# Two transformer layers on one core: key and value loads reordered, phi on GpSimd, and instruction order from a searched list

## The chip, the cores and the metric

The kernel runs on one core of a Trainium2 chip. The metric is device microseconds of one execution. Most executions of one kernel agree within about 0.3%. A profile is one execution, and its "span" is about 1.7 us shorter than the time reported for it.

## The reference

Two layers of a linear-attention block and a gated MLP, on x of 2048 x 512 in bf16:

```python
x = A_x
x = x + _A_ref(_layernorm(x), A_wqkv, A_w_phi, A_wo)      # layer 0
x = x + _B_ref(_layernorm(x), B_W_gate, B_W_up, B_W_down)
x = x + _A_ref(...)                                       # layer 1, same weights
x = x + _B_ref(...)
# _A_ref, 32 heads of 16: q, k, v; phi(k) = [softmax(k w), softmax(-k w)], the same for q;
#   o = phi(q) (phi(k)^T v) / (phi(q) sum(phi(k)));  o @ wo
# _B_ref: (relu(x Wg) * (x Wu)) Wd, with F = 1376
```

## The kernel before

The program is a list of about 2100 operations (`Op`), each with an engine, a cost, a "due" time and its dependences. At build time `plan` simulates the five engines with these costs and emits the operations in the order of the simulated start. Where several operations of an engine could start at the same moment, the one with the smallest due time goes first. `refine` makes the due times: it plans forward, then plans backward from the end, and takes how far before the end each operation must be done as its new due time, ten times over. So its due times are distances to the end along the critical path.

```python
XPOSE = (1200, 2430)       # a DMA transpose: issue, and ns until it has landed
def refine(ops, rounds):
    ...
    for k in range(rounds):
        dues = [o.due for o in ops]
        span = max(o.end for o in plan(ops))
        if best is None or span < best[0]:
            best = span, dues
        back(ops)          # due = -(time left to the end), planned backward
    ...
    return plan(ops)
```

A tile of 128 tokens goes through these steps in a layer (cut):

```python
# normalize (VectorE), then transpose by DMA (or by TensorE for a few early tiles)
xn = (x - mean) * rstd
nc.sync.dma_start_transpose(out=dst(), in_=src.t[:])          # XPOSE
# keys: K = xn^T Wk (4 matmuls of 512 columns), two exps (ScalarE), row sums (VectorE)
# phi = exp * 1/sum, on VectorE, GpSimd, or half each:
if phi_eng == "POOL":  phi(nc.gpsimd, 0, 2)
elif phi_eng == "DVE": phi(nc.vector, 0, 2)
else: phi(nc.vector, 0, 1); phi(nc.gpsimd, 1, 1)              # "BOTH"
# kvz: phi^T [V, 1] summed over all 16 tiles in PSUM
# attend: Eq R (erq), divide (VectorE), transpose o by DMA, output projection (proj), X += ...
# mlp: transpose by DMA, gate and up (G, Up), relu and copy (ScalarE), product (VectorE), down, X += ...
```

Before, phi of layer 0 is "BOTH" for every tile. The transposed tile is needed by TensorE for K, V, proj, G and Up, so a late transpose can stop TensorE.

The softmax here doesn't subtract the row's maximum and nothing guards it: scores larger than these inputs give would overflow.

Of the kernel before, what the change touches and what calls it, by code (L numbers as in the profile page):

```python
# [8 lines left out]
P = 128  # L9
D = 512  # L10
# [138 lines left out]
def back(ops):  # L149


    left = {o: len(o.then) + len(o.behind) for o in ops}
    ready = dict.fromkeys(ops, 0.0)
    clock = dict.fromkeys(HOP, 0.0)
    open_ = {e: [o for o in ops if o.eng == e and not left[o]] for e in HOP}
    for _ in ops:
        best = None
        for e, cand in open_.items():
            if cand:
                at = [(max(clock[e], ready[o] + o.end - o.start - o.spent), o) for o in cand]  # L160
                first = min(t for t, o in at)
                if best is None or first < best[0]:
                    best = first, max((o for t, o in at if t <= first + 1), key=lambda o: (o.start, o.n))
        t, o = best
        clock[o.eng] = t + o.spent
        o.due = -clock[o.eng]
        open_[o.eng].remove(o)
        for d in o.deps:
            left[d] -= 1
            ready[d] = max(ready[d], HOP[o.eng] - o.due)  # L170
            if not left[d]:
                open_[d.eng].append(d)
        for d in o.follow:
            left[d] -= 1
            ready[d] = max(ready[d], d.start + d.spent - d.end - o.due)
            if not left[d]:
                open_[d.eng].append(d)


def refine(ops, rounds):  # L180
    taker = {b: o for o in ops for b in o.takes}
    last = {}
    for o in ops:
        for b in o.takes:
            if b.pool.fifo:
                if b.pool in last:
                    o.follow.append(last[b.pool])
                last[b.pool] = o
    for n, o in enumerate(ops):
        o.n = n  # L190
        o.follow += {taker[b] for b in o.uses} - set(o.deps) - set(o.follow)
        for d in o.deps:
            d.then.append(o)
        for d in o.follow:
            d.behind.append(o)
    best = None
    for k in range(rounds):
        dues = [o.due for o in ops]
        span = max(o.end for o in plan(ops))
        if best is None or span < best[0]:  # L200
            best = span, dues
        back(ops)
    for o, due in zip(ops, best[1]):
        o.due = due
    return plan(ops)
# [4 lines left out]
def mm(n, cols):  # L210
    t = n * (cols / 2.4 + 2.5)
    return t, t + 170
# [24 lines left out]
XPOSE = (1200, 2430)  # L237
RATE = 265.0
# [15 lines left out]
ROUNDS = 10  # L254
BLOCKS = ((1, 1, 2, 2, 2, 2, 2, 2, 2), (1, 1, 2, 2, 2, 2, 2, 2, 1, 1))


@with_exitstack
def kernel(
# [22 lines left out]
    def x_of(t):  # L282
        return X[t // C][:, t % C, :]
# [42 lines left out]
    wqkv = A_wqkv.rearrange("(b p) f -> p b f", p=P)  # L326
    x_in = [None] * T
    x_in[0] = load(0, X[0][:, 0, :], xv[:, 0, :], 131072)
    l_wk = [load(0, wk[:, b:b + 2, :], wqkv[:, b:b + 2, D:2 * D], 262144, "ACT") for b in (0, 2)]
    l_wf = load(1, wf[:], A_w_phi.rearrange("(b j) d f -> (j d) b f", b=NB, j=8), 65536)  # L330
    x_in[1] = load(2, X[0][:, 1, :], xv[:, 1, :], 131072)
    l_wv = load(3, wv[:], wqkv[:, :, 2 * D:3 * D], 524288, "ACT")
    op("ACT", (1300, 1300), 5, lambda: nc.scalar.preload_act_table_set("natural_log_exp_and_others"), name="tbl")
    wov = A_wo.rearrange("(h bb c) f -> c h bb f", bb=NB, c=C)
    gv, uv = (w.rearrange("(b p) f -> p b f", p=P) for w in (B_W_gate, B_W_up))
    dv = B_W_down[0:10 * P, :].rearrange("(f p) d -> p f d", p=P)
    l_wq, l_wo, l_wg, l_wu, l_wd = [], [], [], [], []
    late = [("q", wq[:, b, :], wqkv[:, b, 0:D], 131072) for b in range(NB)]
    late += [("g", wg[:, b, :], gv[:, b, :], 352256) for b in range(NB)]
    late += [("o", wo[i * H:(i + 1) * H, :, :], wov[i], 131072) for i in range(C)]  # L340
    late += [("u", wu[:, b, :], uv[:, b, :], 352256) for b in range(NB)]
    late += [("d", wd[:, f:f + 2, :], dv[:, f:f + 2, :], 262144) for f in range(0, 10, 2)]
    late += [("d", wd[:96, 10, :], B_W_down[10 * P:F, :], 98304)]
    homes = dict(q=l_wq, g=l_wg, o=l_wo, u=l_wu, d=l_wd)

    def load_next(after, due):
        if late:
            kind, dst, src, nbytes = late.pop(0)
            homes[kind].append(load(due, dst, src, nbytes, follow=[after]))
# [29 lines left out]
    def fold(w, dst, loaded, due, step, engs):  # L379
# [10 lines left out]
        for m in range(NB):  # L390
            ps = Buf(p_b)
            f = op("PE", mm(4, 128), due + step + m, lambda m=m, ps=ps: [nc.tensor.matmul(
                ps.t[:, b * P:(b + 1) * P], lhsT=wT.t[:, b, m * P:(m + 1) * P], rhs=Wblk[:, b, :],
                start=True, stop=True) for b in range(NB)], [turned[m], c_blk] + turned[:m], [ps], [wT], name="fold")
            done.append(evac(engs[m % 2], due + step + m, lambda m=m: dst[:, m, :], lambda ps=ps: ps.t[:], [f], (),
                             [ps], "W2"))
# [5 lines left out]
    def turn(src, dst, how, due, after, takes, uses, name):  # L402
        if how == "SP":
            return op("SP", XPOSE, due, lambda: nc.sync.dma_start_transpose(out=dst(), in_=src.t[:]), [after],
                      takes, [src] + uses, name=name, move=500)
        ps = Buf(p_b)
        a = op("PE", mm(4, 128), due, lambda: [nc.tensor.matmul(
            ps.t[:, b * P:(b + 1) * P], lhsT=src.t[:, b * P:(b + 1) * P], rhs=ident[:], start=True, stop=True)
            for b in range(NB)], [after, c_id], [ps], [src], name=name)
        return evac(how, due, dst, lambda: ps.t[:].rearrange("p (b t) -> p b t", b=NB), [a], takes, [ps] + uses,  # L410
                    name)
# [7 lines left out]
    def norm_A(l, t, due, after, how):  # L419
# [11 lines left out]
        return turn(xn, lambda: xnTA[c][:, :, i * P:(i + 1) * P], how, due, n, [], [], "xnTA")  # L431


    class Keys:
# [6 lines left out]
        def tile(self, t, due, due_v, due_z, xT, phi_eng, v_eng="ACT"):  # L441
# [12 lines left out]
                for b in range(NB)], [xT, l_wv], [vp], name="V")  # L454
# [119 lines left out]
    def mlp(l, t0, n, due_x, due_g, due_d, after, how):  # L574
# [3 lines left out]
        turned = []  # L578
        for i in range(n):
            t = t0 + i  # L580
            a = stats(l, "B", t, due_x(i), [after[t]])
            xc = Buf(p_xn)
# [6 lines left out]
            out=tmp[:, t0:t0 + n], in0=mv[:, t0:t0 + n, 1], scalar1=EPS, scalar2=None, op0=Alu.add), [a], name="ve")  # L589
# [44 lines left out]
        for i in range(n):  # L634
            t = t0 + i
            yp = Buf(p_b)
            last = None
            for lo, hi in ((0, 4), (4, 8), (8, NF)):
                def down(yp=yp, i=i, lo=lo, hi=hi):
                    for f in range(lo, hi):  # L640
                        m = min(P, F - f * P)
                        nc.tensor.matmul(yp.t[:], lhsT=h.t[:m, f * W + i * P:f * W + (i + 1) * P],  # L642
                                         rhs=wd[:m, f, :], start=(f == 0), stop=(f == NF - 1))
                last = op("PE", mm(hi - lo, 512), due_d(i) + lo, down,
                          [made[f] for f in range(lo, hi)] + l_wd + ([last] if lo else []),
                          [] if lo else [yp], [yp, h] if lo else [h], name="down")
            x = x_of(t)
            done.append(op("DVE", dve(512, 1, 130), due_d(i), lambda x=x, yp=yp, t=t: nc.vector.scalar_tensor_tensor(  # L648
                out=x, in0=yp.t[:], scalar=rs[:, t:t + 1], in1=x, op0=Alu.mult, op1=Alu.add), [last, r], (), [yp],
                name="resB"))  # L650
# [6 lines left out]
    for t in range(T):  # L657
        if t == 2:
            x_in[2] = load(4, X[0][:, 2, :], xv[:, 2, :], 131072)
            x_in[3] = load(5, X[0][:, 3, :], xv[:, 3, :], 131072)  # L660
        if t >= 4 and t % 2 == 0:
            x_in[t] = x_in[t + 1] = load(
                p["K0"] + p["KS"] * (t - 5), X[t // C][:, t % C:t % C + 2, :], xv[:, t:t + 2, :], 262144,
                follow=[xT[t - 4]] if t > 6 else [])
        xT.append(norm_A(0, t, p["K0"] - 4000 + p["KS"] * t, [x_in[t]], ("ACT", "DVE")[t % 2] if t < 4 else "SP"))
        if t >= 3:
            load_next(xT[t], p["K0"] + p["KS"] * t)
            load_next(xT[t], p["K0"] + p["KS"] * t)
        k0 = p["K0"] + p["KS"] * t
        keys.tile(t, k0, k0 + p["V0"], k0 + p["Z0"], xT[t], "BOTH")  # L670
# [5 lines left out]
    for l in range(2):  # L676
# [18 lines left out]
        for t0, n, s0 in begin:  # L695
# [4 lines left out]
            for i, a in enumerate(done):  # L700
                t = t0 + i
# [5 lines left out]
                else:  # L707
                    op("SP", (460, 1700), e0, lambda t=t: nc.sync.dma_start(
                        out=ov[:, t, :], in_=x_of(t)), [a], name="store",
                       move=131072 / RATE)  # L710
        xT = nxt

    order = refine(ops, ROUNDS)
# [33 lines left out]
```

## Time and profile before

| | before |
|---|---|
| time | 402.70 us, median of 3 runs (402.51 to 403.94) |
| span of the profiled run | 401.2 us |
| TensorE at the measured matmul rates | 380 us of it |

The first lines of the page of the kernel before:

```profile
span 401.2 us, 8365 instructions
PE 387.8 (97%) x3176; PEld 265.9 (66%) x3176; DVE 275.5 (69%) x685; ACT 259.5 (65%) x704; POOL 22.1 (6%) x24
```

A busy TensorE is not yet a full one, since the records of pipelined matmuls overlap (one of 512 columns is recorded as 379 ns). So I use a second measure. In the chain of waits, matmuls in an unbroken row take 216 ns for 512 columns, 109 for 256, and 56 for 128. The sum of all matmuls at these rates, up to a moment, is subtracted from the time up to that moment; this difference is called **shortfall** below. Before, it is 17.8 us by 385 us, and it grows in the first 30 us (10.6), in 60 to 80 (2.7) and in 250 to 300 (2.4).

The busy time by stages, before (columns: window, then busy us and instruction count of TensorE, weight loads, VectorE, ScalarE and GpSimd, then granted clock, share of the DMA engines, GB/s):

```profile
10.00:20.00 10.00, 8.38 (x52) 4.16 (x53) 10.00 (x23) 8.52 (x28) 1.93 (x2) 1.00 0.23 63
20.00:30.00 10.00, 8.40 (x84) 5.32 (x81) 9.88 (x14) 8.02 (x24) 4.86 (x5) 1.00 0.82 190
30.00:40.00 10.00, 9.28 (x57) 4.55 (x56) 9.93 (x23) 8.66 (x28) 2.23 (x2) 1.00 0.73 162
40.00:50.00 10.00, 9.72 (x57) 4.95 (x58) 8.88 (x16) 9.51 (x30) 3.06 (x4) 1.00 0.93 263
```

VectorE is full in 10 to 40 us while TensorE has gaps.

The last lines to keep from before are VectorE and GpSimd around 28 us:

```profile
28.39 1.10 DVE L427 TENSOR_SCALAR xn<-X,mvA,rsA 128x512 bf16<-128x512 bf16 x1
26.68 2.65 POOL L466 TENSOR_TENSOR phiK<-ek,sk 128x512 bf16<-128x512 bf16 x2 [2.55 <-PE q L481]
```

The second of those two GpSimd operations ran from 28.28 to 29.34. The normalization beside it took 1.10 us, where an undisturbed one takes 0.40, and it ended just after GpSimd did.

### The profile page before, as it was taken

What the parts mean: (1) busy time and instruction counts of PE and PEld (TensorE: products, weight loads), DVE (VectorE), ACT (ScalarE), POOL (GpSimd) and SP (SyncE); (2) the same over time, 40 slices, a digit from 0 to 9 for tenths busy, and PEclk for the clock granted to TensorE, in tenths of its full rate; (3) what the DMA queues carried; (4) which work ended last, traced back from release to release, by engine and by line L of the source; (5) the groups of instructions that cost most, each with busy time, mean ns of one, the idle gap of its engine ahead of it and who ended that gap; (6) DMA issues with size and microseconds to landing.
All of it is one profiled execution on the core that took longest, in us unless ns stands there. A gap on an engine that the chain in (4) does not pass through costs nothing.

```text
span 401.2 us, 8365 instructions
## 1 busy us (share of the span) xinstructions
PE 387.8 (97%) x3176; PEld 265.9 (66%) x3176; DVE 275.5 (69%) x685; ACT 259.5 (65%) x704; POOL 22.1 (6%) x24
## 2 busy tenths in 40 slices
PE   6889999899999999999999999999999999999996
PEld 3454565667787678556777845576778686785784
DVE  6999896999995835787365457799998523132222
ACT  4888999977665355838464759997846353452542
POOL 0142350000000000000000002000000000000000
PEclk9999999999999999999999999999999999999999
DMA  6287940233331013101010100025333102001000
GB/s 211 63 192 159 262 118 0 42 67 63 71 68 41 0 28 67 26 15 28 2 26 2 28 0 2 1 41 81 68 65 68 28 26 68 13 29 39 15 28 28
DMA packets 54536, 21.83 MB, mean 54 GB/s; under 512 B 45952, under 2 KB 53472, under 8 KB 54496
## 3 DMA queue, kind: packets, MB, share of 16 engines
q1 hardware_dynamic: 53424, 20.25, 22.4%
q10 hardware_dynamic: 1072, 1.05, 0.8%
q8 instruction: 25, 0.41, 0.4%
q14 instruction: 15, 0.12, 0.1%
HBM read 8.44 MB, written 2.10 MB: 26 GB/s over the span
## 4 chain that ended last, share of the span: by engine, by line
PE 76%; DVE 14%; DMA 4%; ACT 3%; issue 2%; DVEq 0%; ACTq 0%
PE b L607 35%; PE b L642 18%; PE b L452 5%; PE b L446 5%; PE b L565 4%; PE b L518 3%; PE q L481 3%; DMA xnTA<-xn 3%; DVE pr L558 2%; ACT Eq L522 1%; DVE bstA L416 1%; PE q L536 1%; DVE X L569 1%; DVE m L553 1%; DVE o L561 1%
## 5 line engine op out<-in xcount | busy, mean ns | idle before, releaser
L619 ACT ACTIVATE gu<-b 128x512 bf16<-128x512 f32 (+1 forms) x102 | 55.5, 555 | 61.0 <-PE b L607 60.1
L607 PE MATMUL b<-xnTB,wg 128*128 128x256 bf16 (+3 forms) x836 | 92.9, 256 | 0.4 <-ACT Eq L522 0.3
L607 PE MATMUL b<-xnTB,wu 128*128 128x256 bf16 (+3 forms) x836 | 92.9, 256 | 0.2 <-ACT Eq L522 0.2
L625 DVE TENSOR_TENSOR hT<-gu 128x512 bf16<-128x512 bf16 (+1 forms) x102 | 38.5, 380 | 69.2 <-ACT gu L622 69.0
L642 PE MATMUL b<-wd,hT 128*128 128x512 bf16 (+1 forms) x352 | 82.8, 379 | 0.0
L607 PEld LDWEIGHTS <-wg 128*128 128x128 bf16 (+1 forms) x836 | 72.5, 100 | 11.4 <-issue 0.6
L607 PEld LDWEIGHTS <-wu 128*128 128x128 bf16 (+1 forms) x836 | 72.4, 100 | 8.1 <-issue 0.3
L622 ACT CAST gu<-b 128x512 bf16<-128x512 f32 (+1 forms) x102 | 54.8, 543 | 24.7 <-PE b L607 23.4
L642 PEld LDWEIGHTS <-hT 128*128 128x128 bf16 (+1 forms) x352 | 33.8, 98 | 34.8
L543 ACT CAST N<-q 128x384 bf16<-128x384 f32 (+1 forms) x96 | 48.1, 583 | 0.0
L522 ACT ACTIVATE Eq<-b 128x512 bf16<-128x512 f32 x64 | 40.4, 690 | 5.7 <-PE b L518 5.7
L457 DVE TENSOR_REDUCE sk<-ek 128x64 f32<-128x1024 bf16 x32 | 38.6, 1211 | 6.8 <-ACT ek L449 6.7
L648 DVE SCALAR_TENSOR_TENSOR X<-b,rsB,X 128x512 bf16<-128x512 f32 x32 | 23.3, 745 | 27.5 <-PE b L642 27.4
L449 ACT ACTIVATE ek<-b 128x512 bf16<-128x512 f32 x64 | 35.7, 603 | 8.9 <-PE b L446 8.6
L446 PE MATMUL b<-Wk,xnTA 128*128 128x512 bf16 x128 | 32.3, 380 | 4.2 <-DMA xnTA<-xn 2.1
L466 POOL TENSOR_TENSOR phiK<-ek,sk 128x512 bf16<-128x512 bf16 x18 | 21.4, 1193 | 226.6 <-ACT sk L462 221.9
L565 PE MATMUL b<-wo,oT 128*128 128x512 bf16 x128 | 32.5, 379 | 1.1 <-DVE X L569 0.4
L466 DVE TENSOR_TENSOR phiK<-ek,sk 128x512 bf16<-128x512 bf16 (+1 forms) x32 | 31.2, 977 | 2.4 <-ACT sk L462 2.3
L452 PE MATMUL b<-wv,xnTA 128*128 128x512 bf16 x128 | 32.2, 379 | 0.0
L518 PE MATMUL b<-xnTA,Wq 128*128 128x512 bf16 x128 | 31.7, 379 | 0.0
L543 ACT COPY DS<-q 128x48 f32<-128x48 f32 (+1 forms) x96 | 23.7, 318 | 7.2 <-PE q L536 6.1
L536 PE MATMUL q<-R,Eq 128*128 128x144 bf16 x256 | 25.1, 226 | 0.5 <-ACT N L543 0.4
(65 smaller groups left out, 376.1 us busy)
## 6 DMA issues: line engine op xcount, KB each, us to landing
out_dram<-X SPq DMA_DIRECT2D x16, 128.0 KB, 1.7
X<-in_A_x_dram SPq DMA_DIRECT2D x6, 256.0 KB, 4.0
wg<-in_B_W_gate_dram SPq DMA_DIRECT2D x4, 344.0 KB, 3.8
wu<-in_B_W_up_dram SPq DMA_DIRECT2D x4, 344.0 KB, 3.8
wd<-in_B_W_down_dram SPq DMA_DIRECT2D x5, 256.0 KB, 3.1
wk<-in_A_wqkv_dram ACTq DMA_DIRECT2D x2, 256.0 KB, 3.6
X<-in_A_x_dram SPq DMA_DIRECT2D x4, 128.0 KB, 4.4
wv<-in_A_wqkv_dram ACTq DMA_DIRECT2D x1, 512.0 KB, 5.4
```

Of the source, the lines that this page charges most:

```text
L446: k = op("PE", mm(4, 512), due, lambda: [nc.tensor.matmul(kp.t[:], lhsT=xnTA[c][:, b, cols], rhs=Wk2[:, b, :], start=(b == 0), stop=(b == ...
L452: v = op("PE", mm(4, 512), due_v, lambda: [nc.tensor.matmul(vp.t[:], lhsT=xnTA[c][:, b, cols], rhs=wv[:, b, :], start=(b == 0), stop=(b == ...
L457: a = op("DVE", SUM16, due, lambda: nc.vector.tensor_reduce(out=sk.t[:], in_=ek.t[:].rearrange("p s (h f) -> p (s h) f", f=DH), axis=AX.X, ...
L466: e.tensor_tensor(out=ph.t[:, s:s + n].rearrange("p s (h f) -> p (s h) f", f=DH), in0=ek.t[:, s:s + n].rearrange("p s (h f) -> p (s h) f", ...
L518: q = op("PE", mm(4, 512), due(c, b), lambda b=b, qp=qp: [nc.tensor.matmul(qp.t[:], lhsT=Wq2[:, m, b * P:(b + 1) * P], rhs=xnTA[c][:, m, : ...
L522: done.append(op("ACT", act(512), due(c, b), lambda b=b, s=s, qp=qp: nc.scalar.activation(out=Eq[c][:, b, s, :], in_=qp.t[:], func=AF.Exp, ...
L543: nc.scalar.copy(out=q[:, k, 0:3] if k < 2 else q[:, :, 3], in_=ps.t[:, 0:n * GE].rearrange("p (n c j) -> p n c j", n=n, j=HB)[:, :, lo:hi])
L565: a = op("PE", mm(4, 512), due + 3, lambda: [nc.tensor.matmul(yp.t[:], lhsT=oT.t[:, b, :], rhs=wo[:, b, :], start=(b == 0), stop=(b == NB ...
L607: nc.tensor.matmul(ps.t[:m, q * W:(q + 1) * W], lhsT=w[:, b, g * P:g * P + m], rhs=xT.t[:, b, 0:W], start=(b == 0), stop=(b == NB - 1))
L619: nc.scalar.activation(out=gu.t[:m, 0, lo * W:hi * W], in_=gp.t[:m, lo * W:hi * W], func=AF.Relu)
L622: nc.scalar.copy(out=gu.t[:m, 1, lo * W:hi * W], in_=up.t[:m, lo * W:hi * W])
L642: nc.tensor.matmul(yp.t[:], lhsT=h.t[:m, f * W + i * P:f * W + (i + 1) * P], rhs=wd[:m, f, :], start=(f == 0), stop=(f == NF - 1))
```

## The change

Its intent: TensorE starts earlier (value weights first, since V needs no preparation of the weights), VectorE is relieved (phi of layer 0 on GpSimd), loads no longer delay transposes (one per tile instead of two, x further ahead), the end is shorter (last down projection in two column halves), and the order is better (due times from a local search instead of `refine`). Cut to its core:

```diff
-def refine(ops, rounds):          # and back(), removed
+def arrange(ops):
+    assert len(ops) == len(DUE)
...
-        o.n = n
+        o.n, o.due = n, DUE[n]
-XPOSE = (1200, 2430)
-RATE = 265.0
+XPOSE, XPOSE_LOADS = (1200, 2430), (1200, 3500)    # the second for layer 0's xn
+RATE = 320.0
-ROUNDS = 10
+PHI = ["POOL"] * 15 + ["BOTH"]
+DUE = (10365, 18968, 15786, ...)  # 2108 numbers
...
-    l_wk = [load(0, wk..., "ACT") for b in (0, 2)]
+    l_wv = [load(0, wv..., "ACT") for b in (0, 2)]
+    load_x(1, 1, 1)
+    l_wk = [load(1, wk..., "ACT") for b in (0, 2)]
...
-        if t >= 3:
-            load_next(xT[t], ...)
+        if t >= 4:
+            if t % 2 == 0 and t + 4 < T:
+                load_x(t + 4, 2, ..., [xT[t]])
             load_next(xT[t], ...)
-        keys.tile(t, k0, ..., xT[t], "BOTH")
+        keys.tile(t, k0, ..., xT[t], PHI[t])
...
+            halves = ((0, 256), (256, 512)) if l == 1 and t == T - 1 else ((0, 512),)
+            for c0, c1 in halves:          # down, X update and store of each half
```

## The prediction

> **What bounds it now.** TensorE. In the chain that ended last a 512-column matmul costs 216 ns (8 in 1.73 us), a 256-column one 109 ns (88 in 9.61), a 128-column one 56 ns (88 in 4.92). Summed over all 3176 matmuls of the trace at these rates that is about 380 us of the 401.2 us span, so only 21.5 us are not matmul rate. By windows of matmul starts I find them here: 6.3 us before 10 us (plus a warm-up and 1.4 us before it), 2.0 in 10–20, 2.3 in 20–30, 1.1 in 30–40, 0.6 in 40–70, 2.4 in 70–80, 2.4 in 250–270, under 0.2 per 10 us elsewhere, and about 4 us after the last matmul's end (397.06). Nothing the change does to matmul count matters (11 matmuls of 512 columns become 22 of 256); it can only recover these gaps.
>
> **Why the gaps.** In 10–40 us the windows show VectorE at 9.9 of 10 us, ScalarE at 8.0–8.7. A key tile costs VectorE statistics 0.68+0.17, normalization 0.40, row sums 1.21, half of phi 0.68–0.79: 3.2 us, against 2.15 us of matmuls. At the head, the chain goes key weights 5.02, fold, and the first normalized tile is made only at 8.68, although its rsA was ready at 4.63: VectorE was evacuating the fold. Two DMA transposes of 4.13 us (18.79, 36.10) sit in the chain under weight loads; the median is 3.0.
>
> **What moves.**
> 1. Value weights first: the first V needs no fold. xn at about 5.1, transposed by 6, V from about 6.3 instead of 11.1. Key weights land perhaps 1.5 us later, so K starts near 11. Three or four V groups (0.86 us each) fill the head: −2.5 us.
> 2. Phi of 15 tiles wholly on GpSimd: takes 0.7–0.8 us per tile, about 11 us, off VectorE. But GpSimd needs about 2.05 us per tile (two halves of 1.056 us). The Trainium skill, "SBUF — State Buffer", section "SBUF: two separate sides", says GpSimd and VectorE operations with a two-port mode or two SBUF inputs exclude each other for a whole instruction. The trace agrees: the normalization at 28.39, normally 0.40, took 1.10 and ended just after GpSimd's phi. So some of the relief returns as normalizations of up to 2.4 us. I count −2 of the 5.4 us lost in 10–40, together with:
> 3. Loads spread (one per tile, x further ahead): the two 4.1 us transposes come nearer 3: −1 us.
> 4. Transition at 70–80 and 250–270: ScalarE and VectorE are both near full there (19.5 and 16.3 of 20 us in 60–80). Earlier keys and a searched order: −1 us together.
> 5. Last down projection in halves: the final X update, 0.75 us, becomes about 0.45, and the store is smaller: −0.4 us.
>
> Sum −6.9 us; I discount slightly, as the due times come from a model.
>
> **Predicted time: 396.0 us, range 392.0 to 400.5.** Faster by over 2% (below 394.6): 0.33; within 2%: 0.64; slower: 0.03.
>
> **What would show each step.** The first V before 7 us. VectorE below 90% in 10–40, with GpSimd over 60% there, phi about 2 us each and some normalizations over 1 us. Chain with fewer, shorter xnTA transposes. Lost matmul time to 60 us falling from 12 to about 6.5. After 80 us no change except 250–270 and the end. Gap from last matmul to end about 3.7.
>
> **What would make it wrong.** Port exclusion stalling VectorE more than phi freed; GpSimd's longer phi delaying the key sums, and with them the attention; the search paying on the model but not on the chip. Better than predicted, if the searched order closes the transitions entirely (another 3 us).

## More of the kernel before

All comparisons use runs that the record calls fast.

Of the 23 runs of the kernel before that went along with the experiments, the 16 with a granted TensorE clock of 0.999 or 1.000 took 401.6 to 402.5 us, and the 7 with 0.992 to 0.996 took 403.9 to 404.8.

Below, "at full clock" means the runs with at least 0.999; where it changes a verdict, I say so.

What TensorE waited for between 70 and 300 us, before (waits view: total us, times, longest):

```profile
PE b L607 <- ACT Eq L522: 0.4, 2, 0.3
PE b L565 <- DVE X L569: 0.4, 1, 0.4
PE q L536 <- ACT N L543: 0.4, 1, 0.4
PE b L565 <- ACT oT L376: 0.3, 1, 0.3
PE b L446 <- DMA xnTA<-xn: 0.3, 1, 0.3
PE b L565 <- ACT Eq L522: 0.2, 1, 0.2
```

Transposes are hardly there.

## The result

The changed kernel takes 408.31 us (median of 4 runs, 407.98 to 409.23), the kernel before 403.12 in the same rounds. The ratio is 1.0131, with a 95% interval of 1.0104 to 1.0158. Ratios are the mean time of one kernel's fast runs over the mean of the other's in the same rounds, so they are not quite the ratio of the medians quoted. The prediction was 396.0, with a range of 392.0 to 400.5. The change loses 5 us where I expected a gain of 7.

The page of the changed kernel, the lines that answer to those of before:

```profile
span 406.2 us, 8332 instructions
PE 388.7 (96%) x3187; PEld 265.6 (65%) x3187; DVE 272.4 (67%) x671; ACT 260.5 (64%) x704; POOL 33.4 (8%) x24
```

The stages:

```profile
10.00:20.00 10.00, 9.46 (x79) 5.53 (x78) 10.00 (x20) 9.27 (x26) 3.26 (x2) 1.00 0.03 8
20.00:30.00 10.00, 9.59 (x62) 4.92 (x61) 8.17 (x19) 9.70 (x31) 5.63 (x4) 1.00 0.90 215
30.00:40.00 10.00, 9.32 (x60) 4.37 (x57) 10.00 (x15) 7.84 (x28) 5.78 (x4) 1.00 0.88 214
40.00:50.00 10.00, 9.30 (x65) 4.69 (x64) 9.70 (x12) 9.22 (x27) 8.74 (x5) 1.00 0.46 131
```

TensorE is much fuller in 10 to 30 us, as hoped, and emptier than before in 40 to 50. VectorE is again full in 30 to 40, although phi has left it. Its normalizations there, and GpSimd's phi:

```profile
34.21 2.34 DVE L531 TENSOR_SCALAR xn<-X,mvA,rsA 128x512 bf16<-128x512 bf16 x2
38.72 2.35 DVE L531 TENSOR_SCALAR xn<-X,mvA,rsA 128x512 bf16<-128x512 bf16 x2
32.44 3.96 POOL L571 TENSOR_TENSOR phiK<-ek,sk 128x1024 bf16<-128x1024 bf16 x2 [1.62 <-ACT sk L567]
39.00 3.86 POOL L571 TENSOR_TENSOR phiK<-ek,sk 128x1024 bf16<-128x1024 bf16 x2 [2.60 <-ACT sk L567]
```

In each pair of normalizations one took 0.40 us and the other 2.02 or 2.03: it stood behind a whole phi of GpSimd. A third took 1.75 us, at 46.10. What TensorE waited for between 70 and 300 us (the first five of eight lines):

```profile
PE b L670 <- DMA oT<-o: 2.1, 3, 1.3
PE b L551 <- DMA xnTA<-xn: 1.2, 2, 1.0
PE b L557 <- DMA xnTA<-xn: 1.0, 1, 1.0
PE b L670 <- DVE xn L531: 0.8, 1, 0.8
PE q L586 <- DVE phiK L571: 0.6, 1, 0.6
```

DMA transposes head the list now. The fourth line is one too: it is a proj at 95.46 whose transpose landed at 95.41; a wait for several semaphores is put down to one of them. Where the shortfall grew, worked out from the matmul records:

| us of shortfall added in | before | changed |
|---|---|---|
| 0 to 30 | 10.6 | 6.9 |
| 30 to 60 | 1.3 | 4.1 |
| 60 to 80 | 2.7 | 2.3 |
| 80 to 120 | 0.5 | 2.5 |
| 120 to 250 | 0.3 | 3.1 |
| 250 to 300 | 2.4 | 4.0 |
| by 385 in all | 17.8 | 23.0 |

The first 30 us gained 3.7 us. Of that, 2.8 are given back by 60 us. And after 80 us, where the prediction saw "no change except 250-270 and the end", 6.5 us are lost. Seven gaps make up that last part: at 82.9, 94.4, 106.8, 179.8, 214.6, 271.2 and 291.6 us TensorE stood still for 0.78, 0.95, 0.33, 1.12, 1.21, 0.58 and 1.47 us, 6.4 us in sum. In each of them the next group of matmuls starts 0.04 to 0.05 us after a DMA transpose landed. These seven took 2.92 to 4.40 us from issue to landing; the median of the 82 transposes is 2.45.

Late transposes are not new. Before, 11 of the 70 transposes after 60 us took over 2.8 us; in the changed kernel 16 did. But before, TensorE did not need them so soon. The planner can be asked how much time there is in its plan between a transpose landing (after its assumed 2.43 us) and the first matmul that uses it. This is arithmetic on the kernel's own plan, not a measurement:

| | plan | slack under 0.5 us, of 70 transposes after 60 us | span measured | span minus plan |
|---|---|---|---|---|
| before | 396.5 | 2 | 401.2 | 4.7 |
| changed | 392.1 | 17 | 406.2 | 14.1 |

The change took 4.4 us off the plan. Of these, 2.4 are the list's: with its other parts but the old `refine`, the plan is 394.5 us (e1 below). On the chip the plan is wrong by 14 us instead of 5.

**Why a transpose is late.** The Trainium skill, "Runtime: NRT & Kernel Launch", section "Instruction fetch mechanics", says that an engine's instructions are refilled in 16 KiB blocks of 256 instructions over a DMA queue of its own. The trace agrees for TensorE: queue 8 carries 25 packets of 16 KB, one for about every 256 TensorE instructions (6374 matmuls and weight loads). The DMA view of the changed kernel over the transpose that the gap at 291.6 us waited for:

```profile
DMA  9999830000038999969000000000000000018999
GB/s 217 220 212 205 190 53 3 0 0 0 0 50 180 207 227 200 225 147 203 0 0 0 0 0 0 0 0 0 0 0 0 0 0 0 0 40 185 222 212 222
...
q8 instruction: 1, 0.02, 1.6%
```

The window is 289.1 to 293.2 us. The transpose was issued at 289.08; its last packets come some 2 us later, and a fetch packet of 1.02 us starts at 291.02. Fifteen of the sixteen DMA engines reported landing by 2.43 us after issue, the last at 4.14. The skill, "Trainium Kernel Development and Optimization", section "Key Constraints", says that DMAs issued from the SP, ACT and POOL queues all run on the same 16 engines. That the fetch holds up the engine it lands on is my inference from the one late engine of sixteen; in other cases, as the one issued at 91.38, all sixteen are late together, so the mechanism inside the DMA engines stays open. The link itself does not: over all 12 traces in the fast state there are 840 transposes after 60 us; 173 took over 2.8 us, and every one had a fetch packet of 8 or 16 KB in flight between issue and landing; 517 had none, and not one of those was late; 150 had one and were on time. Of the 173, 139 had a 16 KB packet of queue 8; the other 34 had only 8 KB packets of queue 14, a second instruction queue. The traces do not say which engine's it is.

### The profile page after: what moved, and what is told of

It reads as the page before. It is cut to its first block, busy times and chain, and to the rows that moved or that the text cites. A ratio compares the mean times of both kernels' runs of the same rounds, so it can differ in the third digit from the quotient of the medians.

```text
span 406.2 us, 8332 instructions
## 1 busy us (share of the span) xinstructions
PE 388.7 (96%) x3187; PEld 265.6 (65%) x3187; DVE 272.4 (67%) x671; ACT 260.5 (64%) x704; POOL 33.4 (8%) x24
## 5 line engine op out<-in xcount | busy, mean ns | idle before, releaser
L725 ACT ACTIVATE gu<-b 128x512 bf16<-128x512 f32 (+3 forms) x102 | 54.9, 554 | 61.8 <-PE b L713 61.0
L713 PE MATMUL b<-xnTB,wg 128*128 128x256 bf16 (+3 forms) x836 | 90.4, 256 | 0.6 <-ACT xnTB L480 0.6
L749 PE MATMUL b<-wd,hT 128*128 128x512 bf16 (+2 forms) x363 | 83.4, 373 | 0.0
L731 DVE TENSOR_TENSOR hT<-gu 128x512 bf16<-128x512 bf16 (+3 forms) x102 | 38.7, 382 | 62.6 <-ACT gu L728 62.0
L728 ACT CAST gu<-b 128x512 bf16<-128x512 f32 (+3 forms) x102 | 54.3, 541 | 32.7 <-PE b L713 32.1
L571 POOL TENSOR_TENSOR phiK<-ek,sk 128x1024 bf16<-128x1024 bf16 (+1 forms) x18 | 32.7, 1829 | 218.7 <-ACT sk L567 217.5
L648 ACT CAST N<-q 128x384 bf16<-128x384 f32 (+1 forms) x96 | 44.1, 536 | 1.2 <-DVE pr L663 1.1
L756 DVE SCALAR_TENSOR_TENSOR X<-b,rsB,X 128x512 bf16<-128x512 f32 (+1 forms) x33 | 23.2, 730 | 23.4 <-PE b L749 23.4
L627 ACT ACTIVATE Eq<-b 128x512 bf16<-128x512 f32 x64 | 37.4, 664 | 0.9 <-PE b L623 0.6
L641 PEld LDWEIGHTS <-Eq 128*128 128x128 bf16 x256 | 19.4, 98 | 9.0 <-issue 0.9
```

Of the source, the lines that this page charges most:

```text
L571: e.tensor_tensor(out=ph.t[:, s:s + n].rearrange("p s (h f) -> p (s h) f", f=DH), in0=ek.t[:, s:s + n].rearrange("p s (h f) -> p (s h) f", ...
L627: done.append(op("ACT", act(512), due(c, b), lambda b=b, s=s, qp=qp: nc.scalar.activation(out=Eq[c][:, b, s, :], in_=qp.t[:], func=AF.Exp, ...
L641: pe.append(op("PE", mm(len(groups), GE), due, lambda ps=ps, groups=groups: [nc.tensor.matmul(ps.t[:, n * GE:(n + 1) * GE], lhsT=Eq[c][:, ...
L648: nc.scalar.copy(out=q[:, k, 0:3] if k < 2 else q[:, :, 3], in_=ps.t[:, 0:n * GE].rearrange("p (n c j) -> p n c j", n=n, j=HB)[:, :, lo:hi])
L713: nc.tensor.matmul(ps.t[:m, q * W:(q + 1) * W], lhsT=w[:, b, g * P:g * P + m], rhs=xT.t[:, b, 0:W], start=(b == 0), stop=(b == NB - 1))
L725: nc.scalar.activation(out=gu.t[:m, 0, lo * W:hi * W], in_=gp.t[:m, lo * W:hi * W], func=AF.Relu)
```

## The experiments

Theory A: the search spent the slack before transposes, and late transposes then stop TensorE. Rival B: phi on GpSimd, with the port it shares with VectorE, costs the time whatever the order. Rivals C and D are told where they arise. Four kernels ran on a chip together, with the kernel before among them; it took 402.2 to 402.4 us in each of the three batches. All kernels gave correct results.

### Search undone (e1, and again e1b)

```diff
-    order = arrange(ops)
+    order = refine(ops, ROUNDS)     # DUE removed, back() and refine() of before put in
```

> The changed kernel with its list of searched due times taken out and the forward and backward planning of the kernel before put back; loads, phi on GpSimd, halves stay. Theory A (the searched order leaves no slack, so late DMA transposes stop TensorE; the other parts are worth a little): 399 to 402.5 us, faster than the kernel before by 0 to 1%, TensorE gaps over 0.5 us after 70 us sum to under 2 us (changed kernel: about 8). Rival B (phi on GpSimd, with the shared port, slows the kernel, whatever the order): 405 us or more.

Measured: 407.92, 404.10 and 408.37 us, ratio 1.0098 (1.0029 to 1.0167); the profiled run was throttled to a clock of 0.658 (579 us) and says nothing. So undoing the search does not bring the kernel under the kernel before. Theory A's range is missed; Rival B's "405 us or more" fits two of the three runs. None of the three ran at full clock (0.992 to 0.996).

> The first run's kernel once more, for a profile in the fast state (its first was throttled): 404 to 408.5 us. Theory A expects several gaps of TensorE over 0.5 us before an output projection, K or V after 70 us, each behind a transpose of over 3 us; the phi theory expects its loss over before between 20 and 70 us, with normalizations of 1.5 to 2.1 us behind GpSimd's phi.

Measured: 405.33 us (404.44 to 406.77), ratio 1.0062 (1.0017 to 1.0106). The shortfall is 7.1 us by 30, 16.7 by 80, then 17.0 at 120 and 17.0 at 250. So the stalls after 80 us are gone, as they belong to the searched list, and what Theory A expected of this order (several gaps) is wrong: one is left, 0.84 us at 78.5 behind a transpose of 4.54 us. It loses in 30 to 80 us instead: 9.6 us, where the kernel before loses 4.0. About 1.7 of that is the clock, at half speed for 3.41 us from 39.1 us on. The clock does not explain the time, since the two runs at full clock took 405.82 and 406.77 us. Two transposes under weight loads took 5.25 and 6.19 us there (3.5 assumed), and five normalizations took 1.33 to 2.10 us behind GpSimd. That leaves both causes open for the first 80 us. It also means that the list is not the whole loss: without it, the same code is still 3 us or more slower than the kernel before.

### Same searched list, transposes planned as late (e2)

```diff
-XPOSE, XPOSE_LOADS = (1200, 2430), (1200, 3500)
+XPOSE, XPOSE_LOADS = (1200, 4100), (1200, 4100)
```

> The changed kernel with the same due times, but the planner is told that every DMA transpose takes 4.1 us to land (it was 2.43, and 3.5 for layer 0), so the order leaves slack for late ones. Theory A: the stalls of output projections and K or V on a late transpose after 70 us (6.4 us in sum) shrink to under 2 us and the time falls to 401 to 404.5 us. Rival B: no change, 407 to 409 us.

Measured: 399.74 us (399.44 to 399.91), ratio 0.9922 (0.9884 to 0.9960). One assumption of the planner, which changes no operation and no cost on the chip but only the order, is worth 8.6 us against the changed kernel's 408.3 (different rounds). Rival B's "no change" is wrong: phi is on GpSimd here too, and the time fell. Theory A holds, with more than it promised. The seven gaps are 6.4 of the 8.6 us; where the other 2 come from I have not traced. The plan says 392.5 us, only 0.4 longer than the changed kernel's, and it is wrong by 5.1 us, about as before (4.7). In this run, 18 transposes after 60 us were late, more than in the changed kernel; none of TensorE's waits after 70 us is on a transpose. Between 70 and 300 us they are, in full:

```profile
PE q L586 <- DVE phiK L571: 0.6, 1, 0.6
PE b L713 <- ACT xnTB L480: 0.6, 1, 0.6
```

### Instruction fetches shifted (e3)

```diff
-        start=True, stop=True) for _ in range(8)], [c_z], [wps], name="warm")
+        start=True, stop=True) for _ in range(8)] + [nc.tensor.matmul(
+        wps.t[:8, 0:8], lhsT=p_h.tiles[0][:, 0:8], rhs=p_h.tiles[0][:, 0:8],
+        start=True, stop=True) for _ in range(48)], [c_z], [wps], name="warm")
```

> The changed kernel with 48 tiny matmuls (96 TensorE instructions) added to the warm-up; order and data otherwise the same. If transposes are late because TensorE's instruction fetch (one 16 KB packet per 256 TensorE instructions) shares a DMA engine with them, the fetches move by 96 of 256 instructions, some 5 us later or 11 earlier relative to the work: the late transposes at 79.7, 91.4, 176.7, 211.6 and 289.1 us become normal (2.4 to 2.6 us), others become late, each with a fetch inside it; time 403 to 411 us. If lateness comes from the order itself (transposes queued behind each other, or SBUF contention), the same transposes stay late and the same matmul groups wait.

Measured: 407.09 us (406.21 to 407.76), ratio 1.0111. The five named transposes took 2.42, 2.42, 2.59, 2.44 and 2.43 us. Of the 16 that were late in the changed kernel 13 were on time, 9 others were late, and all late ones had a fetch packet inside. Here is the same piece of the program in both, first the changed kernel, then e3 (timeline of TensorE):

```profile
290.93 1.03 PE L670 MATMUL b<-wo,oT 128*128 128x512 bf16 x4
293.26 1.04 PE L670 MATMUL b<-wo,oT 128*128 128x512 bf16 x4 [1.31 <-DMA oT<-o]
```

```profile
289.84 2.07 PE L672 MATMUL b<-wo,oT 128*128 128x512 bf16 x8
```

The two projections that were 1.3 us apart now run without a gap. So which transposes are late is set by where the instruction fetches fall, not by the order of the transposes. All 13 that became punctual had had a packet of queue 8, TensorE's; the three that stayed late (at 104.34, 118.74 and 175.39 us in the changed kernel) had had only one of queue 14. The total falls by only 1.2 us because new places are hit, 0.93 us at 106.0 and 1.50 at 122.4 among them. The second is indirect: VectorE waited 2.29 us for a late transpose (118.53 us, 4.84 us long) before it could normalize and then make the product that TensorE needed. A late transpose thus need not stand in TensorE's own list of waits.

### Slack without the rest (e5)

```diff
-XPOSE = (1200, 2430)          # in the kernel before
+XPOSE = (1200, 4100)
```

> The kernel before, with nothing changed but the latency its planner assumes for a DMA transpose: 4.1 us instead of 2.43. Theory A' (the gain of the second run over before is the searched order plus the new parts, once there is slack): no faster than before, 402 to 405 us, since before lost only about 2 us to late transposes, all in layer 0 and the transitions. Rival C (slack alone gives the gain, the rest of the change nothing): 399 to 400.5 us.

Measured: 405.23 us (404.50 to 407.03), ratio 1.0063 (1.0016 to 1.0109). Rival C falls: slack alone gains nothing; the run at full clock took 404.50 us, still 2 us over before's. Its plan is 1.3 us longer than that of before, and its shortfall is 3 us more by 80 us and the same from there. About 1.7 of these 3 us are the half clock of this one run (3.41 us from 9.9 us on). An order from `refine` has almost no tight transposes after 80 us anyway, so it pays for slack and has nothing to gain from it.

### Phi on GpSimd or shared, with slack (e6, e7), and without (e4)

e6 is e1 with both transposes planned at 4.1 us. e7 and e4 are e6 and e1 with

```diff
-PHI = ["POOL"] * 15 + ["BOTH"]
+PHI = ["BOTH"] * 16
```

> Loads, phi on GpSimd and halves of the changed kernel, planned (not searched), transposes planned at 4.1 us. If late transposes were what made the first run slow, 399 to 402 us; if phi on GpSimd was (normalizations held up by the shared port), still 404 us or more.

> As e6, phi of layer 0 split between VectorE and GpSimd in all 16 tiles. If phi on GpSimd costs time: 2 us or more faster than e6 and no normalization of layer 0 over 1.2 us; if not, within 1.5 us of e6.

> As the first run, but phi of layer 0 split between VectorE and GpSimd again in all 16 tiles. Theory A: within 1.5 us of the first run. Rival B: faster than the first run by 3 us or more.

Measured: e6 401.31 us (ratio 0.9966, 0.9923 to 1.0009), e7 405.01 (1.0051, 1.0006 to 1.0097), e4 404.19 (1.0029, 0.9982 to 1.0076; its profiled run was throttled, 507.6 us, and is left out). e6 lies in the range expected if late transposes, or the lack of slack for them, made the first run slow: slack takes the 405.3 us of e1b to 401.3. With slack, phi on GpSimd is 3.7 us faster, which neither expectation of e7 allowed for. Without slack it is slower: e4's fast runs are 2.8 us below those of e1 from the same rounds (means, 404.0 and 406.8; the medians differ by 4.1). That is not "within 1.5 us", so Theory A's expectation of e4 failed, and Rival B's of 3 us or more about came true. Rival B fails only in "whatever the order", by e2 and by e6 against e7. So slack and the place of phi act together: in the planned orders slack gains 4 us with phi on GpSimd (e1b to e6) and loses 1 to 3 with phi shared (e4 to e7, before to e5). Why is not shown. A searched list without slack and with phi shared was not run. Phi on GpSimd does block normalizations (in e6 three of them took 1.72 to 2.02 us, in e7 none over 1.14), but it takes 13 us of phi off VectorE: 16 operations of 15.3 us in all in e7, one of 2.1 in e6.

### The search repeated, with and without slack (s1, s2), and phi shared (s4)

To see whether the changed kernel's list was just a poor one (Rival D), I searched due times myself: random changes of a few due times, kept when the plan got no longer or, early in a cycle, a little longer; about 600,000 plans each. s1 and s2 have the changed kernel's code with another list. s1 keeps the planner's numbers, s2 has 4.1 us for transposes.

> The changed kernel with due times from a search of my own (some 600,000 plans), started from the planned order of the first run, on the planner's original numbers (transposes land after 2.43 us, 3.5 in layer 0). The planner gives it 391.5 us, less than the changed kernel's 392.1; in its plan 19 of the 70 transposes after 60 us have under 0.5 us before TensorE uses them (changed kernel 17, before 2). Theory A (any search on these numbers spends the slack): 404 to 409 us, although its plan is the shortest; gaps over 0.5 us behind late transposes after 70 us sum to 4 us or more. Rival D (the changed kernel's list is just a poor one): 396 to 400 us.

> The same search with the same effort and start, but with transposes planned at 4.1 us. The planner gives it 392.5 us; no transpose has under 1.6 us of slack at 2.43. Theory A: 397 to 401 us, 5 us or more faster than s1 although its plan is 1 us longer. Rival D: about s1, or slower.

> As s2, with phi of layer 0 split between VectorE and GpSimd in all 16 tiles and its own search: planner 394.2 us, 1.7 more than s2. If phi on GpSimd is worth what e6 and e7 said (3.7 us), 400 to 404 us and slower than s2 by 2 us or more; if that was chance of one order, within 1.5 us of s2.

Measured: s1 404.01 us (402.45 to 406.36), ratio 1.0060 (1.0015 to 1.0105); s2 399.61 (398.89 to 400.19), ratio 0.9932 (0.9916 to 0.9949); s4 401.06 (400.61 to 402.38), ratio 0.9975 (0.9956 to 0.9993). s1 has the shortest plan of all kernels here, 391.5 us, and is no faster than the kernel before: its two runs at full clock took 402.45 and 402.72 us, before's in the same rounds 401.98 to 402.44; its two others, at 0.996, took 405.31 and 406.36. s2, whose plan is a microsecond longer, is 4.4 us faster than s1, or 3.0 at full clock; Theory A had said 5 or more. Rival D's range is missed, but it holds a part: with no more slack than the changed kernel, s1 is 4.3 us faster than it (different rounds). s1 came out at the lower edge of what was expected: gaps of over 0.5 us behind late transposes after 70 us are 1.16, 0.87 and 1.27 us, 3.3 in sum instead of 4. s4 is 1.45 us slower than s2, less than half of what e7 against e6 said, and just within the 1.5 us that I had called the chance of one order. So with slack phi on GpSimd came out 1.5 and 3.7 us faster, and single orders carry a scatter of about that size.

### The version that beats both (s3)

The change's own due list with transposes planned at 4.1 us, searched further from there.

> The second run's kernel (the change's own due times, transposes planned at 4.1 us) with its due times searched a little further: planner 391.95 us after 392.5. Candidate to beat both kernels: 398 to 400.5 us (399.7 in the second run).

Measured: 399.13 us (398.99 to 399.25), ratio 0.9921 (0.9906 to 0.9936). It beats the kernel before by 0.8% and the changed kernel by some 9 us. What TensorE waited for between 70 and 300 us, in full:

```profile
PE q L685 <- ACT N L692: 0.5, 1, 0.5
PE b L555 <- DVE lnB L738: 0.2, 1, 0.2
PE q L685 <- ACT DS L692: 0.2, 1, 0.2
```

Its shortfall is 6.6 us by 30, 10.3 by 60, 12.8 by 80, and then grows by only 1.5 to 385 us.

| kernel | order, assumed landing | phi of layer 0 | plan | span | difference | time | ratio to before |
|---|---|---|---|---|---|---|---|
| before | refine, 2.43 | shared | 396.5 | 401.2 | 4.7 | 402 to 403 | 1 |
| changed | its list, 2.43 | GpSimd | 392.1 | 406.2 | 14.1 | 408.31 | 1.0131 |
| e2 | its list, 4.1 | GpSimd | 392.5 | 397.6 | 5.1 | 399.74 | 0.9922 |
| s3 | its list searched on, 4.1 | GpSimd | 392.0 | 397.4 | 5.4 | 399.13 | 0.9921 |
| e1b | refine, 2.43 | GpSimd | 394.5 | 402.6 | 8.1 | 405.33 | 1.0062 |
| e6 | refine, 4.1 | GpSimd | 394.8 | 399.8 | 5.0 | 401.31 | 0.9966 |
| e7 | refine, 4.1 | shared | 396.6 | 403.2 | 6.6 | 405.01 | 1.0051 |
| e5 | before's, refine, 4.1 | shared | 397.7 | 404.1 | 6.4 | 405.23 | 1.0063 |
| s1 | own search, 2.43 | GpSimd | 391.5 | 400.9 | 9.4 | 404.01 | 1.0060 |
| s2 | own search, 4.1 | GpSimd | 392.5 | 398.4 | 5.9 | 399.61 | 0.9932 |
| s4 | own search, 4.1 | shared | 394.2 | 398.8 | 4.6 | 401.06 | 0.9975 |

(For the changed code, 2.43 means 2.43 and 3.5 for layer 0's xn. The span is that of the one profiled run, the time is the median of all. The spans of e1b and e5 hold about 1.7 us of half clock.)

## Why the prediction was wrong

1. **Value weights first: the mechanism did not happen, a gain came another way, which was luck.** The code lists the value weights first, but the due list then ranks wk before wv, so wk is issued at 0.73 and 1.23 us and wv at 1.75 and 4.09. The first V runs at 8.61 us, not 6.3. In the first 10 us, the head, the shortfall fell by 1.1 us, not 2.5. By 30 us it had fallen by 3.7: the first normalized tile is made at 6.36 instead of 8.68, and 10 to 30 us is much fuller.
2. **Phi on GpSimd: right in kind.** VectorE's own phi in layer 0 fell from 12.6 to 1.5 us; three normalizations took back 4.6 us (2.02, 2.03 and 1.75 against 0.40 each). The skill's "SBUF: two separate sides" (page "SBUF — State Buffer") fits again: a normalization waits for a whole phi. With slack the net was a gain of 1.5 to 3.7 us; without it, a loss of about 3 (e1 against e4).
3. **Loads spread: no gain in the changed kernel.** Of its 12 transposes of xn in layer 0, six took over 2.9 us, the longest 4.22; before, six did, the longest 4.34. In 30 to 60 us the changed kernel loses 2.8 us more than before. Late transposes and a late phi each stop TensorE there; their shares I have not separated. Of the direct waits of TensorE in 10 to 60 us, the profile puts 0.4 us down to a transpose, 0.8 to GpSimd's phi and 1.2 to a copy of V.
4. **The step that failed: "After 80 us no change except 250-270 and the end."** I took the order there as given, because before lost under 0.2 us per 10 us in it. In fact the list reorders the whole program. It cut the slack of transposes to under 0.5 us in 17 of 70 cases (2 before), and seven late ones cost 6.4 us, more than the whole loss of 5. I had named "the search paying on the model but not on the chip" among the risks, but gave it almost no weight: a range that ends at 400.5, below the kernel before, and a discount of well under 1 us.
5. **Signs in the profile.** I had asked for VectorE below 90% in 10 to 40 us and GpSimd over 60% there; they were 94% (10.00, 8.17 and 10.00 of 10) and 49% (3.26, 5.63 and 5.78). Lost matmul time by 60 us was to fall from 12 to 6.5 and fell to 11.0. The place to look was the list of waits after 70 us, which I had not asked for.
6. **Transitions:** 60 to 80 us gained 0.4; 250 to 300 lost 1.6 more instead, with two of the seven gaps in it (0.58 and 1.47 us). I had said 1 us less in all.
7. **The end:** from the start of the last matmul to the end of the span it was 3.87 us before and 3.33 after (starts at 397.31 and 402.86); the gain is 0.5, and the 0.4 that I said was about right.

With slack put back, the same change takes 399.7 us, inside the predicted range. That does not make the prediction right: the time asked for was that of the list as delivered.

## What to carry to other kernels

If a program's order comes from a simulated plan, a search on that plan can spend the slack that the plan's numbers say is free: here 17 and 19 of 70 transposes were left with under 0.5 us, where `refine` had left 2. So before a search, plan the operations whose duration varies (here DMA transposes, 2.4 to 4.8 us after 60 us) at their bad duration, not their median. It cost 0.4 us of plan and saved 8.6 us on the chip for the delivered list, and 3 to 4.4 us in my own search; in the unsearched order of the kernel before it saved nothing. Compare the plan with the trace, operation by operation, before and after a search: an error that grows is the search fitting the model. And an engine stage that was without gaps before is no proof that it will be after a reordering.

## What the Trainium skill lacked or had wrong

- "Runtime: NRT & Kernel Launch", section "Instruction fetch mechanics", calls the cost of crossing a 16 KiB boundary "mostly hidden". For the engine itself no run here contradicts that: in s3, 22 such packets fell after 70 us, and the longest wait of TensorE there was 0.5 us. But the page does not say that the fetch packet delays other DMAs: a transpose of 2.45 us took up to 4.8 us when a fetch fell into it (after 60 us, 173 late of 323 with a fetch, 0 of 517 without), and in the changed kernel this stopped TensorE for 6.4 us.
- The same section does not mention that adding instructions moves the stalls: 96 more TensorE instructions at the start made 13 of 16 late transposes punctual and 9 others late.
- No page that I used gives the spread of a DMA transpose under weight loads: 2.4 to 6.2 us in the first 60 us of these traces.
